# A fused attention and mixture kernel: first batch's q remainder loaded apart and finished late, later batches' loads pinned in the plan, last sub-tile's products, sums and stores rearranged

## The chip, the cores and the metric

The kernel runs on one core of one Trainium2 chip. The metric is the device time of one execution in microseconds (us), median of several runs. A run's time is about 1.8 us more than the span that its profile shows (first to last instruction): the profiled run of the kernel before took 510.41 us and its span is 508.6 us. Below, "time" is the first, "span" the second.

PE is the matrix engine (TensorE), DVE is VectorE, ACT is ScalarE, POOL is GpSimd, SP is SyncE, which here only issues DMAs.

## The reference

```python
# q, k, v: 8 batches, 8 heads, 576 positions, 64 wide
phi = lambda x: where(x > 0, x, exp(x) - 1) + 1
kv  = einsum('bhsd,bhse->bhde', phi(k), v);  z = phi(k).sum(axis=2)
x   = einsum(phi(q), kv) / (einsum(phi(q), z) + 1e-6)     # -> x: 4608 x 512
# mixture: 4 experts, w1 512 x 1024, w2 1024 x 512
p   = domain_probs / (domain_probs.sum(-1) + 1e-9)
out = sum over e of p[:, e] * (relu(x @ w1[e]) @ w2[e])
```

## The kernel before

A batch of 576 positions is cut into 512 and a remainder of 64. The attention goes by pairs of heads, four per batch. Each pair loads k, v and q, takes exp on ACT, maps on DVE, then PE makes kv, the numerators and denominators, and DVE divides. The remainders of k, v and q of a batch are loaded for all heads at once. The first 512 positions go through the four experts while the weights arrive. Everything after that is 64 "units" of 256 rows and one expert: seven block products instead of eight in each layer (a Strassen-like scheme), about 6.18 us of PE each.

Each operation is handed to a small planner with an engine, an assumed duration, a priority and its dependencies. The planner simulates the machine once, at build time, and from that comes one fixed order for each engine.

```python
def order(self):
    ...                                   # pick the engine that can start first
        n = min((n for n, x in cand.items() if x <= t + self.NEAR),
                key=lambda n: (ops[n]["pri"], n))
        start[n] = max(t, at[n])          # at[n]: ready time; begins at o["after"]
        free[e] = done = start[n] + o["dur"]
        if o["move"]:                     # a DMA: assumed time to landing
            mover = max(done + 1.2, mover) + o["move"]
            done = mover + 0.8
    ...                                   # POOL keeps the order of the program
```

For a load of a pair (issue 0.5, move 0.7) the plan thus assumes a landing 0.5 + 1.2 + 0.7 + 0.8 = 3.2 us after the start of the issue when no other DMA is in the way. On the chip no planned time is enforced. Only the order is, and each engine waits at its next instruction until its inputs are there.

The parts that the change touches:

```python
def load_rest(b, queue, pri):                      # k, v, q remainders, together
    for i, (t, o) in enumerate(((k, kqr[rs, 0]), (v, vr[rs]), (q, kqr[rs, 1]))): dma(...)

def rest_maps(b, pe_mode, pri):                    # one exp over k and q together
    pl.add("ACT", 1.05, pri, lambda: nc.scalar.activation(er[rs], kqr[rs], AF.Exp), ...)

def batch(b):                                      # batches 2 to 7, beside the units
    due = U(8 * (b - 1)) - 8                       # U(n) = 84 + 6.4 n
    for pr in range(DC):
        t = due - (DC - pr) * 2 * TU
        load_pair(b, pr, "SP", t - 12)             # a priority only, no earliest time
        if pr == 0:
            load_rest(b, "SP", t - 12); rest_maps(b, False, t - 6)
        attention(b, pr, False, t, 1.7)

# last unit of a sub-tile: seven products, then four sums and the stores
seq = (P1, P4, P5, P2, P6, P7, P3)
ACT: s15 = l2b[0]                                  # after P1 and P5
DVE: of[0:2] = l2b[1] + s1;  of[2] = l2b[3] + of[1]
DVE: of[1,3] = of[1,2] + s5; of[1:3] = l2b[2] + of[1:3]
SP : four stores of 128 KB, one after the other    # last sub-tile
```

Of the kernel before, what the change touches and what calls it, by code (L numbers as in the profile page):

```python
# [109 lines left out]
def kernel(  # L110
# [10 lines left out]
    nc = tc.nc  # L121
# [24 lines left out]
    def sb(name, shape, dt):  # L146
        return pc.tile(shape, dt, tag=name, name=name)

    identh = sb("identh", [P, P], FP16)
    w1_sb = [sb(f"w1_{e}", [P, DC, F], FP16) for e in range(E)]  # L150
# [31 lines left out]
    xr_sb = sb("xr_sb", [P, B // 2, Dm], FP16)  # L182

    kqs.append(
        xp_a.bitcast(FP32).rearrange("p a c (x d) -> p a (c x) d", d=D)
# [35 lines left out]

    def dma(queue, pri, out_, in_, w, move, r=(), hold=False, mark=False):

        eng = nc.gpsimd if queue == "POOL" else nc.sync

        def go():
            i = eng.dma_start(out=out_, in_=in_)
            if mark:
                last["mark"] = i.ins.name
            if hold:  # L230
                tc.add_manual_dep(
                    i.ins,
                    last["mark"],
                    mybir.DependencyInfo(
                        mybir.DependencyClass.Sync, mybir.DependencyReason.DATA
                    ),
                    reason="load order",
                )

        pl.add(  # L240
            queue,
            0.72 if queue == "POOL" else 0.5,
            pri,
            go,
            r=r + (("mark",) if hold else ()),
            w=w + (("mark",) if mark else ()),
            move=move,
        )

    stage = {}  # L250

    def load_pair(b, pr, queue, pri):
        hs = slice(2 * pr, 2 * pr + 2)
        n = 3 if b < 2 else 2
        i = rot("stage%d" % n, n) if n == 2 else rot("stage3", 3)
        stage[b, pr] = i
        kk = stage_keys(i)
        for t, o, key in ((k, kqs[i][:, 0], kk[0]), (v, vss[i], kk[2]), (q, kqs[i][:, 1], kk[1])):
            dma(queue, pri, o, t[b, hs, 0:NT].rearrange("h (p c) d -> p h c d", c=C), (key,), 0.7, hold=b == 2)

    def load_rest(b, queue, pri):
        par = b % 2
        rs = slice(par * R, par * R + R)
        for i, (t, o) in enumerate(((k, kqr[rs, 0]), (v, vr[rs]), (q, kqr[rs, 1]))):
            dma(queue, pri, o, t[b, :, NT:S].rearrange("h s d -> s h d"), (("str", par, i),), 0.75, hold=b in (2, 3))

# [36 lines left out]

    def rest_maps(b, pe_mode, pri):
        par = b % 2
        rs = slice(par * R, par * R + R)
        ei = rot("ek", 2)
        er = ek_b[ei].rearrange("p i h c d -> p i (h c) d")
        ek = (("ek", ei, 0), ("ek", ei, 1))
        s_ = [("str", par, i) for i in range(3)]  # L310

        def maps(i):
            o = kqpr[rs, i]
            nc.vector.tensor_scalar(o, kqr[rs, i], 0.0, 1.0, AO.max, AO.add)
            nc.vector.tensor_tensor(out=o, in0=er[rs, i], in1=o, op=AO.min)

        pl.add("ACT", 1.05, pri, lambda: nc.scalar.activation(er[rs], kqr[rs], AF.Exp),
               r=(s_[0], s_[2]), w=ek)
        pl.add("ACT", 0.55, pri + 0.1,
               lambda: nc.scalar.copy(vprs[par][rs, :, 0:D], vr[rs]), r=(s_[1],), w=(("vpr", par),))  # L320
        for i, key in enumerate(("kpr", "qpr")):
            pl.add("DVE", 0.92, pri + 0.5, lambda i=i: maps(i), r=(s_[0], s_[2]) + ek, w=(key,))
        if not pe_mode:
            pl.add("SP", 0.45, pri + 1, lambda: nc.sync.dma_start_transpose(
                out=qTr[par][:, :, rs], in_=kqpr[rs, 1].rearrange("p h d -> p (h d)")),
                r=("qpr",), w=[("qTr", par, i) for i in range(DC)], move=1.2)

    def attention(b, pr, pe_mode, pri, step, two=False):
# [15 lines left out]
        vp = vps[vi]  # L344
        zi = rot("kvz", 2)
        kvz = kvs[zi]
# [17 lines left out]
        if pe_mode:  # L364

            tq, tk = (l2b[1].bitcast(FP16), "l2b1") if two else (tbank, "l2b3")

            def turn():
                for c in range(C):
                    nc.tensor.transpose(  # L370
                        out=tq[:, c * P : (c + 1) * P], in_=qp[:, c], identity=identh
                    )
                nc.tensor.transpose(
                    out=tq[:, NT : NT + R],
                    in_=kqpr[rs, 1, hs].rearrange("p h d -> p (h d)"),
                    identity=identh[rs, rs],
                )

            pl.add("PE", 0.32, pri + 3 * step, turn, r=(("kqp", pi, 1), "qpr", "ident"),
                   w=(tk,))  # L380
            pl.add("ACT", 0.5, pri + 3.5 * step, lambda: nc.scalar.copy(
                qT.rearrange("p c t -> p (c t)"), tq[:, 0:NT]), r=(tk,), w=(("qT", ti),))
            pl.add("DVE", 0.2, pri + 3.5 * step, lambda: nc.vector.tensor_copy(
                qTr[par][:, pr, rs], tq[:, NT : NT + R]), r=(tk,), w=(("qTr", par, pr),))
        else:
            pl.add("SP", 0.45, pri + 3 * step, lambda: nc.sync.dma_start_transpose(
                out=qT, in_=qp.rearrange("p c h d -> p (c h d)")),
                r=(("kqp", pi, 1),), w=(("qT", ti),), move=1.2)
# [43 lines left out]
        def norm(u, c0, n, ri):  # L432
            nd = at[:, 0 : n * 2 * DE]
            if two and u:
                nd = l2b[2][:, 2 * DE : 6 * DE]
            nd = nd.rearrange("p (c h e) -> p c h e", c=n, h=2)
# [8 lines left out]
            )  # L445
            if c0:
                nc.vector.tensor_tensor(
# [5 lines left out]

        for u, (c0, n) in enumerate(((0, 3), (3, 2))):
            ri = rot("rc", 2)
            pl.add("PE", 0.06 * n, pri + (5 + u) * step, lambda u=u, c0=c0, n=n: nd_mm(u, c0, n),
                   r=(("qT", ti), ("qTr", par, pr), ("kvz", zi)), w=ndk[u])
            pl.add("DVE", (0.72, 0.74)[u], pri + (5.5 + u) * step,
                   lambda u=u, c0=c0, n=n, ri=ri: norm(u, c0, n, ri), r=ndk[u],
                   w=[("x", par, pr, c) for c in range(c0, min(c0 + n, C))]  # L460
                   + ([("xr", b, pr)] if u else []))

# [291 lines left out]
    def l2_unit(n):  # L754
# [25 lines left out]
        P3 = (2, 0, s4[:, 3], Q(3), quad(e, 1, 1), KW(1, 1), False)  # L780
        seq = (P1, P4, P5, P2, P6, P7, P3)
        if first:
            seq = (P1, P5, P2, P6, P7, P4, P3)
        p0 = U(n + 1) + 0.45
        for i, (bank, half, a, ak, w, wk, opens) in enumerate(seq):
            pl.add("PE", 0.436, p0 + 0.9 * i,
                   lambda bank=bank, half=half, a=a, w=w, opens=opens: prod(bank, half, a, w, opens),
                   r=(ak,) + wk, w=lk(bank))
        if not last:
# [7 lines left out]
        s1, s5 = (s15[:, i : i + 1].broadcast_to([P, 2, HD]) for i in range(2))  # L797
        pl.add("ACT", 0.5, p0 + 3.5, lambda: nc.scalar.copy(
            s15.rearrange("p a d -> p (a d)"), l2b[0]), r=("l2b0",), w=("s15",))
        pl.add("DVE", 0.62, p0 + 4.5, lambda: tt(  # L800
# [11 lines left out]
        else:  # L812
            for u in range(2):
                for par in range(2):
                    b = 2 * (2 * s + u) + par
                    dma("SP", p0 + 9, out[b * S + NT : (b + 1) * S, :],
                        ot[par * R : (par + 1) * R, u, :], (), 0.5, r=r)

# [9 lines left out]
    consts(0)  # L828
    pl.add("DVE", 0.8, 5, lambda: consts(1), w=(("vp", 1), ("vpr", 1), ("kvz", 1)))
    for i in range(2):  # L830
        pl.add("DVE", 0.27, 6 + 30 * i, lambda i=i: nc.vector.memset(qTr[i], 0.0),
               w=[("qTr", i, pr) for pr in range(DC)])
    load_pair(0, 0, "SP", 0)
    load_rest(0, "POOL", 0)
    load_pair(0, 1, "POOL", 0)
    load_w1(0, (0,))
    load_pair(0, 2, "POOL", 0)
    load_w1(0, (1,))
    rest_maps(0, True, 3)
    for pr in range(DC):  # L840
        if pr == 3:
            load_pair(0, 3, "POOL", 0)
            load_w1(0, (2, 3))
            probs()
        attention(0, pr, True, 2.5 + 4 * pr, 0.4, two=True)
        turn_x(pr, 6 + 4 * pr)
    load_w2(0)
    load_w1(1, range(DC))
# [28 lines left out]
    def batch(b):  # L877

        due = U(8 * (b - 1)) - 8
        for pr in range(DC):  # L880
            t = due - (DC - pr) * 2 * TU
            load_pair(b, pr, "SP", t - 12)
            if pr == 0:
                load_rest(b, "SP", t - 12)
                rest_maps(b, False, t - 6)
            attention(b, pr, False, t, 1.7)

# [54 lines left out]
```

## Time and profile before

| | before |
|---|---|
| time, first three runs | 508.58 us (508.37 to 508.60) |
| span of the profiled run | 508.6 us |
| PE busy | 484.1 us, 95% |
| first layer 1 product | 16.73 us |
| continuous layer 1 products from | 28.21 us |
| last matmul ends, then the span ends | 501.28, 508.64 us |

The page's summary of busy time of the kernel before:

```profile
span 508.6 us, 14922 instructions
PE 484.1 (95%) x6008; PEld 425.0 (84%) x6008; DVE 410.6 (81%) x1035; ACT 367.1 (72%) x685; POOL 42.6 (8%) x68
```

Busy time does not say how densely PE works, because the records of matmuls overlap: one of 256 columns is 273 ns long (page of before, L765), and the densest start every 109 ns. I therefore worked out a second number from the trace, used all through this document: the "PE excess" of a stretch. It is the sum over matmuls of the time from one start to the next, less what the columns would take at a yardstick of 2.4 per ns, 457.0 us for the whole program. The yardstick is a round number, chosen a little above the densest that the traces show: a product of 512 columns every 0.216 us (2.37 per ns), one of 256 every 0.109 us (2.35). Below, "streaming" is time by this yardstick. So not all excess could be gained: the densest units, after 400 us, take 6.18 us for 5.97 us of streaming. At 0.21 us for each of the 40 units begun between 120 and 380 us, some 8.4 us of excess in that stretch are a floor (an estimate). The first matmul's start, the streaming, the excess and the tail add up to the span.

The timeline of the kernel before, at the start (start us, length us, engine, line, what; in brackets how long the engine was idle and what ended it):

```profile
9.21 1.06 ACT L317 ACTIVATE ek<-kqr 64x1024 f16<-64x1024 f32 x1 [0.30 <-DMA kqr<-in_q_dram]
11.27 0.42 DVE L315 TENSOR_TENSOR kqpr<-ek,kqpr 64x512 f16<-64x512 f16 x1
16.73 1.44 PE L537 MATMUL l1b<-s,w 128*128 128x512 f16 x3 [0.15 <-ACT s L532]
24.02 0.27 DVE L289 TENSOR_REDUCE prs<-p 128x32 f32<-128x128 f32 x1
28.21 1.36 PE L537 MATMUL l1b<-s,w 128*128 128x512 f16 x3 [0.67 <-ACT s L532]
```

The first line is one exp over the k and q remainders, waiting for the q remainder's load. The first layer 1 product comes at 16.73 us, and products run without gaps only from 28.21 us. From 24.02 us DVE does the arithmetic of the probabilities.

The timeline of the kernel before, at the end:

```profile
500.68 0.60 PE L765 MATMUL l2b<-w,s 128*128 128x256 f16 x4
501.30 0.42 DVE L802 TENSOR_TENSOR ot<-l2b,ot 128x256 f32<-128x256 f32 x1
501.75 0.69 DVE L805 TENSOR_TENSOR ot<-ot,s 128x512 f32<-128x512 f32 x1
502.55 0.69 DVE L807 TENSOR_TENSOR ot<-l2b,ot 128x512 f32<-128x512 f32 x1
503.27 2.39 SPq L227 DMA_DIRECT2D out_dram<-ot  x4
```

After the last product DVE still has three sums, then one queue issues four stores in 2.39 us.

ACT's waits in the middle of the kernel before, 120 to 380 us (who waited for whom, total us, times, longest), the four lines in which it waited for DMAs or longest for PE:

```profile
ACT h L703 <- PE l1b L689: 17.4, 17, 2.0
ACT kvz L413 <- PE at L403: 15.1, 15, 1.8
ACT xp L649 <- DMA xT<-xp: 0.6, 2, 0.4
ACT ek L358 <- DMA kq<-in_k_dram: 0.6, 2, 0.4
```

ACT waits for PE there, which is as it should be when PE is the limit, and hardly for loads (0.6 us for k).

### The profile page before, as it was taken

Reading aid. Unit: us, or ns where it says so; the run is one execution under the profiler, and the core shown is the slowest. Engines: PE = TensorE matmul, PEld = TensorE weight load, DVE = VectorE, ACT = ScalarE, POOL = GpSimd, SP = SyncE. Lnnn points to the kernel's source line nnn. Section 1 sums busy time; section 2 is a strip of 40 time slices with the busy share of each in tenths; the row PEclk is TensorE's granted clock in tenths of the full one; section 3 lists DMA queues with packets and bytes.
Section 4 is the critical chain, followed back from the end, with each engine's and each line's share of the span. In section 5 each row is a group of like instructions: output and inputs, shape, how many; then the busy total and the mean of one; then the engine's idle time right before and its main releaser. Section 6 shows DMA issues by size and latency. Waiting matters only on the chain.

```text
span 508.6 us, 14922 instructions
## 1 busy us (share of the span) xinstructions
PE 484.1 (95%) x6008; PEld 425.0 (84%) x6008; DVE 410.6 (81%) x1035; ACT 367.1 (72%) x685; POOL 42.6 (8%) x68
## 2 busy tenths in 40 slices
PE   1889999999999999999999999999999999999994
PEld 0534454889999999999999999999999999999993
DVE  5867897889998989898988989799868676666754
ACT  5636658887987699768977897778666766666640
POOL 8756500000000000000000000000000000000000
PEclk9989999999999999999999999999999999999999
DMA  8999988995775678555665565645322432323311
GB/s 233 227 232 225 262 164 188 234 201 136 162 182 120 138 145 177 121 137 129 175 112 136 124 147 141 108 113 105 95 43 75 54 84 44 84 48 80 51 35 43
DMA packets 124006, 67.51 MB, mean 133 GB/s; under 512 B 94480, under 2 KB 117776, under 8 KB 123936
## 3 DMA queue, kind: packets, MB, share of 16 engines
q1 hardware_dynamic: 115216, 51.79, 46.9%
q0 software_dynamic: 8720, 14.76, 13.7%
q8 instruction: 47, 0.77, 0.7%
q14 instruction: 23, 0.19, 0.1%
HBM read 45.16 MB, written 9.44 MB: 107 GB/s over the span
## 4 chain that ended last, share of the span: by engine, by line
PE 85%; ACT 5%; DMA 4%; DVE 2%; issue 2%; POOL 0%; POOLq 0%; DVEq 0%; ACTq 0%
PE l1b L689 37%; PE l2b L765 36%; PE l2b L547 4%; PE l1b L537 4%; DMA kq<-in_k_dram 2%; PE at L424 2%; PE at L400 1%; DMA kqr<-in_q_dram 1%; ACT xp L649 1%; ACT ek L358 1%; DMA w<-in_moe_w_dram 1%; ACT h L703 1%; ACT l1b L706 1%; ACT p L706 0%; DVE x L440 0%
## 5 line engine op out<-in xcount | busy, mean ns | idle before, releaser
L689 PEld LDWEIGHTS <-w 128*128 128x128 f16 x2048 | 132.9, 98 | 5.6 <-issue 1.0
L765 PE MATMUL l2b<-w,h 128*128 128x256 f16 x768 | 115.1, 273 | 0.3 <-ACT h L703 0.2
L765 PE MATMUL l2b<-t,s 128*128 128x256 f16 x768 | 112.6, 273 | 0.0
L703 ACT ACTIVATE h<-l1b 128x512 f16<-128x512 f32 x128 | 76.7, 599 | 43.1 <-PE l1b L689 41.1
L689 PEld LDWEIGHTS <-w1x 128*128 128x128 f16 x1536 | 100.1, 98 | 5.5 <-issue 2.1
L765 PEld LDWEIGHTS <-s 128*128 128x128 f16 x1024 | 91.2, 98 | 7.1 <-DVE s L751 0.2
L709 DVE CUSTOM_DVE_ANT_0 h<-l1b,p 128x512 f16<-128x512 f32 x64 | 44.2, 691 | 50.1 <-PE l1b L689 48.5
L689 PE MATMUL l1b<-xT,w 128*128 128x128 f16 x1024 | 78.1, 219 | 0.8 <-ACT l1b L706 0.7
L689 PE MATMUL l1b<-xs,w1x 128*128 128x128 f16 x1024 | 77.9, 219 | 0.9 <-DVE h L709 0.4
L689 PE MATMUL l1b<-xs,w 128*128 128x128 f16 x1024 | 78.0, 219 | 0.0
L649 ACT ACTIVATE xp<-x,p_nat 128x512 f16<-128x512 f16 x112 | 76.6, 724 | 0.7 <-DMA xT<-xp 0.6
L765 PEld LDWEIGHTS <-h 128*128 128x128 f16 x768 | 67.3, 98 | 5.4 <-ACT h L703 0.9
L751 DVE TENSOR_TENSOR s<-h 128x512 f16<-128x512 f16 x128 | 53.8, 421 | 1.6
L706 ACT COPY u<-l1b 128x512 f32<-128x512 f32 x64 | 37.5, 586 | 16.0 <-PE l1b L689 15.8
L709 DVE CUSTOM_DVE_ANT_0 h<-l1b,u 128x512 f16<-128x512 f32 x64 | 43.7, 682 | 0.8 <-ACT h L703 0.5
L706 ACT COPY l1b<-l1b 128x512 f32<-128x512 f32 x64 | 36.8, 575 | 10.4 <-PE l1b L689 9.6
L706 ACT COPY p<-l1b 128x512 f32<-128x512 f32 x64 | 37.3, 583 | 7.9 <-PE l1b L689 6.7
L667 DVE TENSOR_TENSOR xs<-xT,xs 128x256 f16<-128x256 f16 x128 | 37.0, 289 | 5.1 <-PE l1b L689 0.5
L358 ACT ACTIVATE ek<-kq 128x512 f16<-128x512 f32 x60 | 37.8, 631 | 3.3 <-DMA kq<-in_k_dram 2.3
L689 PE MATMUL l1b<-xT,w1x 128*128 128x128 f16 x512 | 39.0, 219 | 0.0
L765 PE MATMUL l2b<-w,s 128*128 128x256 f16 x256 | 38.4, 273 | 0.0
L537 PE MATMUL l1b<-s,w 128*128 128x512 f16 x124 | 31.1, 399 | 1.4 <-ACT s L532 1.2
(99 smaller groups left out, 561.0 us busy)
## 6 DMA issues: line engine op xcount, KB each, us to landing
w<-in_moe_w_dram POOLq DMA_DIRECT2D x32, 256.0 KB, 7.3
out_dram<-ot SPq DMA_DIRECT2D x16, 512.0 KB, 2.8
kq<-in_k_dram SPq DMA_DIRECT2D x25, 256.0 KB, 3.3
vs<-in_v_dram SPq DMA_DIRECT2D x25, 256.0 KB, 2.9
kq<-in_q_dram SPq DMA_DIRECT2D x25, 256.0 KB, 3.2
kq<-in_k_dram POOLq DMA_DIRECT2D x5, 256.0 KB, 7.2
vs<-in_v_dram POOLq DMA_DIRECT2D x5, 256.0 KB, 6.6
kq<-in_q_dram POOLq DMA_DIRECT2D x5, 256.0 KB, 6.0
```

Of the source, the lines that this page charges most:

```text
L358: pl.add("ACT", 0.55, pri + i * step, lambda i=i: nc.scalar.activation(ek[:, i], kq[:, i], AF.Exp), r=(sk[i],), w=(("ek", ei, i),))
L424: nc.tensor.matmul(out=nds[u][c - c0], lhsT=qT[:, c] if c < C else qTr[par][:, pr], rhs=kvz, start=True, stop=True,)
L537: nc.tensor.matmul(out=bank, lhsT=w1_sb[e][:, dc, fj * P : (fj + 1) * P], rhs=xt0[:, dc, :], start=(dc == 0), stop=(dc == DC - 1),)
L547: nc.tensor.matmul(out=bank, lhsT=hts[ht[fj]][:, c * P : (c + 1) * P], rhs=w2_sb[e][:, fj, :], start=(fj == 0), stop=(fj == FC - 1),)
L649: pl.add("ACT", 0.55, pri, lambda c=c, src=src, ps=ps: nc.scalar.activation(xp[:, c, :], src, AF.Copy, scale=ps), r=r, w=(("xp", xi, c),))
L667: lambda o=o, a=a, b_=b_: tt(out=o, in0=a, in1=b_, op=AO.subtract),
L689: nc.tensor.matmul(out=bank[:, fc * P : (fc + 1) * P], lhsT=wt[:, kc, fc * P : (fc + 1) * P], rhs=r[:, kc, :], start=(start and fc == 0 an ...
L703: return lambda: nc.scalar.activation(o, bank, AF.Relu)
L706: return lambda: nc.scalar.copy(o, bank)
L709: return lambda: nc.vector._custom_dve(TENSOR_ADD_SAT, out=o, in0=bank, in1=t, s0=BIG, s1=0.0)
L751: pl.add("DVE", 0.36, U(n + 1) + d - 0.5, lambda i=i, a=a, b_=b_, alu=alu: tt(out=s4[:, i], in0=a, in1=b_, op=alu), r=r, w=(Q(i),))
L765: nc.tensor.matmul(out=l2b[bank][:, half * HD : (half + 1) * HD], lhsT=a[:, c, :], rhs=w[:, c], start=(opens and first and c == 0), stop=( ...
```

## The change

Its intent: start the dense work of PE sooner, shorten what follows the last matmul, and move the attention of the later batches to where ACT and DVE have room. The diff, cut to its core (the identity matrix and two more kv buffers are also laid over `s15`, which is free until the first sub-tile's sums, and the exp of the k and q remainders is split in two in all batches):

```diff
-    load_rest(0, "POOL", 0)
+    load_rest(0, "POOL", 0, parts=(0, 1))            # k and v remainders first
     ...
-    rest_maps(0, True, 3)
+    rest_maps(0, True, 3, (0,))
     for pr in range(DC):
         if pr == 3:
             load_pair(0, 3, "POOL", 0)
             load_w1(0, (2, 3))
+            load_rest(0, "POOL", 0, parts=(2,))      # q remainder here
             probs()
         attention(0, pr, True, 2.5 + 4 * pr, 0.4, two=True)   # without the remainder
+    rest_maps(0, True, 30, (1,))
+    rest_late(32)      # turn, products and divisions of all four pairs' remainders
 ...
 def batch(b):
     due = U(8 * (b - 1)) - 8
     for pr in range(DC):
         t = due - (DC - pr) * 2 * TU
-        load_pair(b, pr, "SP", t - 12)
+        if b == 2:
+            t = T0 + 4 + 10.5 * pr
+        load_pair(b, pr, "SP", t - 8, after=t - 8)   # "after": planned no earlier
         if pr == 0:
-            load_rest(b, "SP", t - 12)
-            rest_maps(b, False, t - 6)
-        attention(b, pr, False, t, 1.7)
+            load_rest(b, "SP", t - 7, after=t - 7)
+            rest_maps(b, False, t - 2)
+        attention(b, pr, False, t, 1.5)
 ...
+    elif end:                                        # the last unit of all
+        seq = (P1, P5, P6, P7, P4, P2, P3)
 ...
+    if end:   # six sums, each as soon as its product is there; two stores early,
+              # two at the end, each two from SP and ACT side by side
```

More of the change, by code (lines that the diff above doesn't have):

```diff
@@ L147, in sb @@
         return pc.tile(shape, dt, tag=name, name=name)
-    identh = sb("identh", [P, P], FP16)
     w1_sb = [sb(f"w1_{e}", [P, DC, F], FP16) for e in range(E)]
@@ L182 @@
     xr_sb = sb("xr_sb", [P, B // 2, Dm], FP16)
+    s15h = s15.rearrange("p a d -> p (a d)").bitcast(FP16)
+    identh = s15h[:, 0:P]
+    kvs += [
+        s15h[:, P + i * 2 * DE : P + (i + 1) * 2 * DE].rearrange("p (h e) -> p h e", h=2)
+        for i in range(2)
+    ]
     kqs.append(
@@ L220, with dma @@
     last = {}
-    def dma(queue, pri, out_, in_, w, move, r=(), hold=False, mark=False):
-        eng = nc.gpsimd if queue == "POOL" else nc.sync
+    def dma(queue, pri, out_, in_, w, move, r=(), hold=False, mark=False, after=0.0):
+        eng = {"POOL": nc.gpsimd, "SP": nc.sync, "ACT": nc.scalar}[queue]
         def go():
@@ L247, in dma, with load_pair @@
             move=move,
+            after=after,
         )
     stage = {}
-    def load_pair(b, pr, queue, pri):
+    def load_pair(b, pr, queue, pri, after=0.0):
         hs = slice(2 * pr, 2 * pr + 2)
@@ L258, in load_pair, with load_rest @@
         for t, o, key in ((k, kqs[i][:, 0], kk[0]), (v, vss[i], kk[2]), (q, kqs[i][:, 1], kk[1])):
-            dma(queue, pri, o, t[b, hs, 0:NT].rearrange("h (p c) d -> p h c d", c=C), (key,), 0.7, hold=b == 2)
-    def load_rest(b, queue, pri):
+            dma(queue, pri, o, t[b, hs, 0:NT].rearrange("h (p c) d -> p h c d", c=C), (key,), 0.7,
+                hold=b == 2, after=after)
+    def load_rest(b, queue, pri, after=0.0, parts=(0, 1, 2)):
         par = b % 2
         rs = slice(par * R, par * R + R)
-        for i, (t, o) in enumerate(((k, kqr[rs, 0]), (v, vr[rs]), (q, kqr[rs, 1]))):
-            dma(queue, pri, o, t[b, :, NT:S].rearrange("h s d -> s h d"), (("str", par, i),), 0.75, hold=b in (2, 3))
+        for i in parts:
+            t, o = ((k, kqr[rs, 0]), (v, vr[rs]), (q, kqr[rs, 1]))[i]
+            dma(queue, pri, o, t[b, :, NT:S].rearrange("h s d -> s h d"), (("str", par, i),), 0.75,
+                hold=b in (2, 3), after=after)
     def load_w1(e, dcs):
@@ L301, in probs, with rest_maps @@
                r=(("prawr", 0), ("prawr", 1)), w=("prest",))
-    def rest_maps(b, pe_mode, pri):
+    def rest_maps(b, pe_mode, pri, parts=(0, 1)):
         par = b % 2
@@ L308, in rest_maps @@
         er = ek_b[ei].rearrange("p i h c d -> p i (h c) d")
-        ek = (("ek", ei, 0), ("ek", ei, 1))
-        s_ = [("str", par, i) for i in range(3)]
         def maps(i):
@@ L315, in maps @@
             nc.vector.tensor_tensor(out=o, in0=er[rs, i], in1=o, op=AO.min)
-        pl.add("ACT", 1.05, pri, lambda: nc.scalar.activation(er[rs], kqr[rs], AF.Exp),
-               r=(s_[0], s_[2]), w=ek)
-        pl.add("ACT", 0.55, pri + 0.1,
-               lambda: nc.scalar.copy(vprs[par][rs, :, 0:D], vr[rs]), r=(s_[1],), w=(("vpr", par),))
-        for i, key in enumerate(("kpr", "qpr")):
-            pl.add("DVE", 0.92, pri + 0.5, lambda i=i: maps(i), r=(s_[0], s_[2]) + ek, w=(key,))
+        for i in parts:
+            sk, ek, key = ("str", par, 2 * i), ("ek", ei, i), ("kpr", "qpr")[i]
+            pl.add("ACT", 0.55, pri + i * 0.5, lambda i=i: nc.scalar.activation(
+                er[rs, i], kqr[rs, i], AF.Exp), r=(sk,), w=(ek,))
+            if i == 0:
+                pl.add("ACT", 0.55, pri + 0.1, lambda: nc.scalar.copy(
+                    vprs[par][rs, :, 0:D], vr[rs]), r=(("str", par, 1),), w=(("vpr", par),))
+            pl.add("DVE", 0.92, pri + 0.5 + i * 0.5, lambda i=i: maps(i), r=(sk, ek), w=(key,))
         if not pe_mode:
@@ L326, in rest_maps, with rest_late, turn, mm @@
                 r=("qpr",), w=[("qTr", par, i) for i in range(DC)], move=1.2)
+    def rest_late(pri):
+        rs = slice(0, R)
+        def turn():
+            for pr in range(DC):
+                nc.tensor.transpose(
+                    out=tbank[:, pr * R : (pr + 1) * R],
+                    in_=kqpr[rs, 1, 2 * pr : 2 * pr + 2].rearrange("p h d -> p (h d)"),
+                    identity=identh[rs, rs],
+                )
+        pl.add("PE", 0.22, pri, turn, r=("qpr", "ident"), w=("l2b3",))
+        pl.add("DVE", 0.3, pri, lambda: nc.vector.tensor_copy(
+            qTr[0][:, :, rs], tbank[:, 0 : DC * R].rearrange("p (a t) -> p a t", a=DC)),
+            r=("l2b3",), w=[("qTr", 0, pr) for pr in range(DC)])
+        for p0, n in ((0, 3), (3, 1)):
+            ri = rot("rc", 2)
+            def mm(p0=p0, n=n):
+                for pr in range(p0, p0 + n):
+                    nc.tensor.matmul(
+                        out=slot[pr - p0], lhsT=qTr[0][:, pr], rhs=kvs[pr], start=True, stop=True
+                    )
+            def norm(p0=p0, n=n, ri=ri):
+                nd = at[rs, 0 : n * 2 * DE].rearrange("p (c h e) -> p c h e", c=n, h=2)
+                rc = rc_b[ri][rs]
+                nc.vector.reciprocal(rc[:, 0:n], nd[:, :, :, D:DE])
+                nc.vector.tensor_tensor(
+                    out=xr_sb[rs, 0, p0 * P : (p0 + n) * P].rearrange(
+                        "p (c h d) -> p c h d", c=n, h=2
+                    ),
+                    in0=nd[:, :, :, 0:D],
+                    in1=rc[:, 0:n].broadcast_to([R, n, 2, D]),
+                    op=AO.mult,
+                )
+            prs = range(p0, p0 + n)
+            pl.add("PE", 0.06 * n, pri + 1, mm,
+                   r=[("qTr", 0, pr) for pr in prs] + [("kvz", pr) for pr in prs], w=("at",))
+            pl.add("DVE", 0.25 + 0.16 * n, pri + 1.5, norm, r=("at",),
+                   w=[("xr", 0, pr) for pr in prs])
     def attention(b, pr, pe_mode, pri, step, two=False):
@@ L344, in attention @@
         vp = vps[vi]
-        zi = rot("kvz", 2)
+        zi = pr if two else rot("kvz", 2)
         kvz = kvs[zi]
@@ L372, in turn @@
                     )
+                if two:
+                    return
                 nc.tensor.transpose(
@@ L377, in turn @@
                 )
-            pl.add("PE", 0.32, pri + 3 * step, turn, r=(("kqp", pi, 1), "qpr", "ident"),
-                   w=(tk,))
+            pl.add("PE", 0.32, pri + 3 * step, turn,
+                   r=(("kqp", pi, 1), "ident") + (() if two else ("qpr",)), w=(tk,))
             pl.add("ACT", 0.5, pri + 3.5 * step, lambda: nc.scalar.copy(
                 qT.rearrange("p c t -> p (c t)"), tq[:, 0:NT]), r=(tk,), w=(("qT", ti),))
-            pl.add("DVE", 0.2, pri + 3.5 * step, lambda: nc.vector.tensor_copy(
-                qTr[par][:, pr, rs], tq[:, NT : NT + R]), r=(tk,), w=(("qTr", par, pr),))
+            if not two:
+                pl.add("DVE", 0.2, pri + 3.5 * step, lambda: nc.vector.tensor_copy(
+                    qTr[par][:, pr, rs], tq[:, NT : NT + R]), r=(tk,), w=(("qTr", par, pr),))
         else:
@@ L434, in norm @@
             if two and u:
-                nd = l2b[2][:, 2 * DE : 6 * DE]
+                nd = l2b[2][:, 2 * DE : (2 + 2 * n) * DE]
             nd = nd.rearrange("p (c h e) -> p c h e", c=n, h=2)
@@ L445, in norm @@
             )
-            if c0:
+            if n == 2:
                 nc.vector.tensor_tensor(
@@ L452, in norm @@
                 )
-        for u, (c0, n) in enumerate(((0, 3), (3, 2))):
+        for u, (c0, n) in enumerate(((0, 3), (3, 1 if two else 2))):
             ri = rot("rc", 2)
             pl.add("PE", 0.06 * n, pri + (5 + u) * step, lambda u=u, c0=c0, n=n: nd_mm(u, c0, n),
-                   r=(("qT", ti), ("qTr", par, pr), ("kvz", zi)), w=ndk[u])
-            pl.add("DVE", (0.72, 0.74)[u], pri + (5.5 + u) * step,
+                   r=(("qT", ti), ("kvz", zi)) + ((("qTr", par, pr),) if n == 2 else ()), w=ndk[u])
+            pl.add("DVE", (0.5, 0.74, 0.72)[n - 1], pri + (5.5 + u) * step,
                    lambda u=u, c0=c0, n=n, ri=ri: norm(u, c0, n, ri), r=ndk[u],
                    w=[("x", par, pr, c) for c in range(c0, min(c0 + n, C))]
-                   + ([("xr", b, pr)] if u else []))
+                   + ([("xr", b, pr)] if n == 2 else []))
     out_t = [
@@ L781, in l2_unit @@
         seq = (P1, P4, P5, P2, P6, P7, P3)
+        end = n == nu - 1
         if first:
             seq = (P1, P5, P2, P6, P7, P4, P3)
+        elif end:
+            seq = (P1, P5, P6, P7, P4, P2, P3)
         p0 = U(n + 1) + 0.45
@@ L787, in l2_unit @@
                    lambda bank=bank, half=half, a=a, w=w, opens=opens: prod(bank, half, a, w, opens),
-                   r=(ak,) + wk, w=lk(bank))
+                   r=(ak,) + wk, w=lk(bank) + ((("p", bank, half),) if end else ()))
         if not last:
@@ L797, in l2_unit, with store @@
         s1, s5 = (s15[:, i : i + 1].broadcast_to([P, 2, HD]) for i in range(2))
-        pl.add("ACT", 0.5, p0 + 3.5, lambda: nc.scalar.copy(
-            s15.rearrange("p a d -> p (a d)"), l2b[0]), r=("l2b0",), w=("s15",))
+        sk = ("s15", "ident", ("kvz", 2), ("kvz", 3))
+        if end:
+            for i in range(2):
+                pl.add("ACT", 0.36, p0 + i, lambda i=i: nc.scalar.copy(
+                    s15[:, i], l2b[0][:, i * HD : (i + 1) * HD]), r=(("p", 0, i),),
+                    w=(("s15", i),) + (() if i else sk))
+        else:
+            pl.add("ACT", 0.5, p0 + 3.5, lambda: nc.scalar.copy(
+                s15.rearrange("p a d -> p (a d)"), l2b[0]), r=("l2b0",), w=sk)
+        stores = [(u, par) for u in range(2) for par in range(2)]
+        def store(u, par, queue, r):
+            b = 2 * (2 * s + u) + par
+            dma(queue, p0 + 9, out[b * S + NT : (b + 1) * S, :],
+                ot[par * R : (par + 1) * R, u, :], (), 0.3, r=r)
+        if end:
+            lo, hi = (lambda bank: l2b[bank][:, 0:HD]), (lambda bank: l2b[bank][:, HD : 2 * HD])
+            for dur, o, a_, b_, r, w in (
+                (0.4, of[:, 0], hi(1), s15[:, 0], (("p", 1, 1), ("s15", 0)), (O(0),)),
+                (0.3, of[:, 1], of[:, 0], s15[:, 1], (("s15", 1),), (O(0),)),
+                (0.62, of[:, 2:4], lo(3)[:, None].broadcast_to([P, 2, HD]), of[:, 0:2],
+                 (("p", 3, 0), O(0)), (O(2),)),
+                (0.4, of[:, 2], hi(2), of[:, 2], (("p", 2, 1),), (O(2),)),
+                (0.4, of[:, 0], lo(1), s15[:, 0], ("l2b1",), (O(0),)),
+                (0.4, of[:, 1], lo(2), of[:, 1], lk(2), (O(0),)),
+            ):
+                i = cnt.get("lp", 0)
+                cnt["lp"] = i + 1
+                pl.add("DVE", dur, p0 + 2 + i * 0.5,
+                       lambda o=o, a_=a_, b_=b_: tt(out=o, in0=a_, in1=b_, op=AO.add), r=r, w=w)
+                if i in (3, 5):
+                    for par, queue in enumerate(("SP", "ACT")):
+                        store(int(i == 3), par, queue, (O(2 if i == 3 else 0),))
+            return
         pl.add("DVE", 0.62, p0 + 4.5, lambda: tt(
@@ L812, in l2_unit @@
         else:
-            for u in range(2):
-                for par in range(2):
-                    b = 2 * (2 * s + u) + par
-                    dma("SP", p0 + 9, out[b * S + NT : (b + 1) * S, :],
-                        ot[par * R : (par + 1) * R, u, :], (), 0.5, r=r)
+            for u, par in stores:
+                store(u, par, "SP", r)
     def consts(i):
@@ L829 @@
     pl.add("DVE", 0.8, 5, lambda: consts(1), w=(("vp", 1), ("vpr", 1), ("kvz", 1)))
+    pl.add("DVE", 0.4, 5, lambda: [nc.vector.memset(kvs[i], 0.0) for i in (2, 3)],
+           w=(("kvz", 2), ("kvz", 3)))
     for i in range(2):
```

## The prediction

> **What bounds the kernel now.** The matrix engine (PE): the summary of busy time says 484.1 of 508.6 us (95%), the chain of waits is 85% PE. From 32 to 501.3 us PE is dense: [...] except where the change works:
>
> 1. Start, 0 to 32 us (excess about 18 us). First layer 1 product at 16.73 us, continuous products only from 28.21. The chain runs through the q remainder: it lands at 9.12, one exp over k and q (1.06 us) waits for both, VectorE maps k (ready 10.72), then q, then turn, qT copy, products, x. Later VectorE's probability arithmetic (24.02 to 26.13) stands before the last pair's norm, and PE runs at half clock from 28.3 to 31.7 (512 columns take 427 ns, not 216).
> 2. Main stage's beginning, 84 to 116 us: excess 4.7 us where 1.1 is normal. ScalarE and VectorE are 80 to 90% busy with batch 2's attention and the first units; PE waits for copies.
> 3. Tail: last matmul ends 501.29, sums until 503.24, four stores issued by one queue 503.27 to 505.66, last landing 507.43, end 508.64.
>
> **What the change does.**
> - Start: the q remainder's load leaves the queue's head (1.5 us between landings), its half of the exp (0.5 us), its maps (1.0), and per pair a turn, a 0.19 us copy, a product and a 0.27 us norm leave the pair chain. They come back once, later: about 0.6 us ScalarE, 2.5 VectorE, under 1 PE. Pair 0 then hangs on its q load (8.25): first layer 1 product near 14 us, continuous ones near 24.5. [...] Weights land early enough; tight are batch 1's remainders (41.8 to 43.1). I keep 3.3 us, range 1.5 to 5.5.
> - Main stage: batch 2's loads and attention are planned 5 to 12 us later, off the crowded 80 to 100 us: 1.5 us, range -0.5 to 3. Other batches' later loads cost nothing.
> - Tail: the new product order has its operands in time. Six sums (five of 256 columns, 0.42; one of 512, 0.69) start after the third product and end about 1.15 us after the last matmul instead of 1.95. Two stores go earlier; the last two are issued together, so the last issue begins 1.25 us after the last matmul instead of 3.8. Landing (2.3) and ending (1.2) stay: 2.6 us saved, range 2.1 to 3.
>
> **Sum.** All on the critical path: 3.3 + 1.5 + 2.6 = 7.4; predicted 501.2 us, 8 in 10 within 497.8 to 504.5. Faster by over 2%: 0.17; within: 0.82; slower: 0.01.
>
> **Right or wrong would show as:** first layer 1 product at 13.5 to 15 us; dense PE from 23.5 to 26; first unit's product 3 us earlier than 87.3; excess in 84 to 116 under 3.5; last matmul to end 4.7 us (7.35 before).
>
> **What would make it wrong:** the static order puts the late remainder's turn or norms before work PE needs; load landings in 10 to 50 us (queue saturated) hold the earlier PE back; batch 2's delayed loads starve its units near 135 us; or the probability arithmetic still delays the last pair.

The forecast's sum came to 3.3 + 1.5 + 2.6 = 7.4 us, which takes the median of 508.58 us to 501.2. In the start's paragraph was a reason to hope for up to 1.7 us more, half of the 3.4 us that the trace shows at half clock (28.3 to 31.7 us). The text does not say how much of that is in the 3.3 us or in the range's upper end of 5.5. The excess is defined above, and from 120 to 380 us it is 9.9 us, or 0.76 us per 20 us. Where the text calls a queue saturated, 10 to 50 us, the trace has the DMA engines at a busy share of 1.13 (the packets' time, summed, over the time of 16 engines).

## The result

| | before | changed |
|---|---|---|
| time, first job | 508.59 us (4 runs) | 508.06 us (4 runs, 506.77 to 508.72) |
| time, second job | 508.82 us (11 runs) | 509.03 us (7 runs, 507.94 to 513.09) |
| span, two traces each | 508.6 and 506.7 us | 506.0 and 511.2 us |

The profiled run of before (510.41 us) is none of these; it was 1.8 us above the median of the first three. The ratio of the first job is 0.9986 (95% interval 0.9965 to 1.0007), of the second 0.9994 (0.9972 to 1.0017): the same. A ratio here is the mean time of one kernel's fast runs over that of the other's of the same rounds, so it is not quite the ratio of the medians above. 501.2 us had been predicted, 497.8 to 504.5.

Yet the trace shows the gains. The page's summary and the timeline of the changed kernel, at the start:

```profile
span 506.0 us, 14856 instructions
PE 483.4 (96%) x6008; PEld 424.3 (84%) x6008; DVE 409.1 (81%) x1036; ACT 368.3 (73%) x694; POOL 43.0 (8%) x68
```

```profile
6.51 0.63 ACT L327 ACTIVATE ek<-kqr 64x512 f16<-64x512 f32 x1 [2.15 <-DMA kqr<-in_k_dram]
15.31 1.44 PE L594 MATMUL l1b<-s,w 128*128 128x512 f16 x3 [0.29 <-ACT s L589]
23.93 0.81 PE L594 MATMUL l1b<-s,w 128*128 128x512 f16 x3 [0.68 <-ACT s L589]
```

The exp of the k remainder starts 2.7 us earlier and is shorter, the first product comes 1.4 us earlier and the continuous ones 4.3 us earlier (23.93 for 28.21).

The timeline of the changed kernel at the end:

```profile
499.97 0.60 PE L822 MATMUL l2b<-w,s 128*128 128x256 f16 x4
501.12 0.41 DVE L888 TENSOR_TENSOR ot<-l2b,s 128x256 f32<-128x256 f32 x1
501.23 1.13 SPq L232 DMA_DIRECT2D out_dram<-ot  x2
501.23 1.39 ACTq L232 DMA_DIRECT2D out_dram<-ot  x2
501.45 0.41 DVE L888 TENSOR_TENSOR ot<-l2b,ot 128x256 f32<-128x256 f32 x1
```

The last matmul ends at 500.57 and the span at 506.03, so the tail is 5.46 us where it was 7.36.

So far so good, but the last matmul ends only 0.7 us earlier. The lead over the first trace of before, by the start of each unit's first product (worked out from the timelines):

| unit | 0 | 2 | 8 | 16 | 32 | 44 | 63 |
|---|---|---|---|---|---|---|---|
| lead, us | 5.08 | 9.19 | 5.46 | 4.80 | 2.42 | 0.54 | 0.71 |

(The drop from 9.19 to 5.46 is partly no loss: batch 2's attention was moved into these units, and PE has to do it there. How large that part is was not worked out.) From unit 8 to unit 44 the lead melts away, a little in each batch. ACT's waits of the changed kernel, 120 to 380 us, the lines with a DMA as releaser:

```profile
ACT ek L412 <- DMA kq<-in_q_dram: 3.1, 6, 0.9
ACT ek L412 <- DMA kq<-in_k_dram: 2.6, 4, 1.0
ACT vp L408 <- DMA vs<-in_v_dram: 2.1, 2, 1.2
ACT xp L706 <- DMA xT<-xp: 1.1, 1, 1.1
ACT ek L327 <- DMA kqr<-in_q_dram: 0.5, 1, 0.5
```

Together 9.4 us where it was 1.2 in the kernel before. ACT makes the copies out of PSUM that PE needs, in the same fixed order, so a late load stops these copies as well (in the case below ACT waits 3.46 us for a load, and PE then 3.01 us for a copy). In the changed kernel's first trace 18 matmuls between 120 and 380 us, the first at 128 and the last at 362, start over 0.12 us late by the count of excess. In the first trace of before 3 do. The second trace of the changed kernel (511.2 us) shows one such case in full. SP's issues, then ACT and PE:

```profile
220.87 0.57 SPq L232 DMA_DIRECT2D kq<-in_k_dram  x1
221.50 0.47 SPq L232 DMA_DIRECT2D vs<-in_v_dram  x1
222.02 0.47 SPq L232 DMA_DIRECT2D kq<-in_q_dram  x1
222.58 0.41 SPq L232 DMA_DIRECT2D out_dram<-ot  x1
223.04 0.63 SPq L232 DMA_DIRECT2D kqr<-in_k_dram  x1
223.71 1.48 SPq L232 DMA_DIRECT2D vr<-in_v_dram  x1
225.23 1.41 SPq L232 DMA_DIRECT2D kqr<-in_q_dram  x1
```

```profile
228.81 0.22 PE L481 MATMUL at<-kvz,qTr 128*128 128x130 f16 x1
229.14 0.63 ACT L408 CAST vp<-vs 128x512 f16<-128x512 f32 x1 [3.46 <-DMA vs<-in_v_dram]
231.41 0.57 ACT L763 COPY l1b<-l1b 128x512 f32<-128x512 f32 x1
232.03 0.61 PE L746 MATMUL l1b<-xs,w1x 128*128 128x128 f16 x8 [3.01 <-ACT l1b L763]
232.95 1.06 PE L746 MATMUL l1b<-xT,w 128*128 128x128 f16 x8
```

The v load issued at 221.50 is one of seven DMAs that SP issued within 5.8 us (220.87 to 226.64), one of them a store of 512 KB. ACT waits 3.46 us for it (it landed at 229.12, 7.6 us after the issue), waits another 0.36 us for the q load, then works through an exp, a relu and the copy that PE's next product needs, and PE stands for 3.01 us. This is the worst case of both traces. In the first trace the same load, in the same company, landed in 5.0 us, and PE's starts were late by at most 0.52 us. What made it 2.6 us slower the second time is not shown. After that PE's clock is halved: eight products of 128 columns take 0.85 us (232.95 to 233.80) instead of 0.44. The granted clock of the same run in that stretch (the columns are: stretch, length, then busy us and instructions of PE, PEld, DVE, ACT and POOL, the granted clock, the DMA engines' share and GB/s):

```profile
229.00:232.00 3.00, 0.03 (x1) 0.00 (x0) 0.59 (x2) 2.44 (x5) 0.00 (x0) 1.00 0.09 23
232.00:236.30 4.30, 4.27 (x36) 3.76 (x36) 3.23 (x10) 4.17 (x8) 0.00 (x0) 0.60 0.02 4
```

In this trace ACT kept its order: PE's last layer 1 products before the stall had ended by 228.5 us, yet the relu at 230.78 and the copy at 231.41 us that read such products stood behind the cast at 229.14.

The traces by stretch, in us of PE excess (for "start", the time to the first matmul plus the excess up to 80 us). "Waits" is ACT's idle time of over 0.2 us that a DMA ended, 120 to 380 us, counted by me and so not to the tenth the sum of the views' lines:

| | start | 80-120 | 120-380 | after 380 | tail | waits |
|---|---|---|---|---|---|---|
| before, first trace | 25.2 | 4.9 | 9.9 | 4.1 | 7.36 | 0.9 |
| before, second trace | 22.8 | 5.0 | 10.3 | 4.0 | 7.39 | 1.3 |
| changed, first trace | 20.5 | 3.0 | 15.8 | 4.1 | 5.46 | 9.5 |
| changed, second trace | 20.6 | 3.0 | 20.8 | 4.2 | 5.34 | 12.8 |

### The profile page after: what moved, and what is told of

Same layout as the page of the kernel before. It is cut to its first block, busy times and chain, and to the rows that moved or that the text cites. A ratio compares the mean times of both kernels' runs of the same rounds, so it can differ in the third digit from the quotient of the medians.

```text
span 506.0 us, 14856 instructions
## 1 busy us (share of the span) xinstructions
PE 483.4 (96%) x6008; PEld 424.3 (84%) x6008; DVE 409.1 (81%) x1036; ACT 368.3 (73%) x694; POOL 43.0 (8%) x68
## 4 chain that ended last, share of the span: by engine, by line
PE 72%; ACT 9%; DMA 7%; DVE 7%; issue 4%; SPq 2%; DVEq 0%; POOL 0%; POOLq 0%; ACTq 0%
PE l1b L746 29%; PE l2b L822 28%; PE l1b L594 6%; PE l2b L604 5%; DMA kq<-in_q_dram 2%; ACT xp L706 1%; ACT h L760 1%; SPq L232 1%; DMA kqr<-in_q_dram 1%; PE at L481 1%; DVE s L808 1%; DMA xT<-xp 1%; ACT ek L412 1%; DMA kqr<-in_k_dram 1%; PE at L457 1%
## 5 line engine op out<-in xcount | busy, mean ns | idle before, releaser
L405 DVE TENSOR_TENSOR kqp<-ek,kqp 128x512 f16<-128x512 f16 x64 | 27.2, 425 | 7.7 <-ACT ek L412 3.6
```

The costliest lines, as they stand in the source:

```text
L405: nc.vector.tensor_tensor(out=o, in0=ek[:, i], in1=o, op=AO.min)
```

## The experiments

Theory A: the pinned loads of the later batches, planned close before their use, arrive late on the chip; ACT waits for them in its fixed order, PE starves, and the lead is given back. Theory B: the lead can't be held, whatever the loads do, because ACT, DVE or the DMA engines have no room in the attention stretches. Rival C: the finer steps of 1.5 or batch 2's new place are the cause, and the late loads are only seen beside it.

Every edit of the plan shuffles the fixed order of all engines a little, so a single experiment says less than several that agree. Each run left one trace, and the changed kernel's own two differ by 5.0 us of excess in 120 to 380 us. The ratios, from five or six timed runs of each experiment but two, are therefore the firmer evidence. All differences are below 2%. What tells the experiments from no change is that their 95% intervals do not reach 1.

### All later batches planned as before

The changed kernel with `batch()` of the kernel before (t - 12, no `after`, steps of 1.7, batch 2 not moved).

> The changed kernel with the later batches' loads and attention planned as before (loads 12 us ahead of the attention, steps of 1.7, batch 2 not moved). Theory A (the moved loads of batches 2 to 7 arrive late, ScalarE waits for them in order, PE starves, and the lead won at the start is given back): most of the lead of the start stays, 499 to 503 us. Theory B (the lead is lost whatever the schedule of the loads, as ScalarE, VectorE or the DMA engines can't go faster in the attention stretches): 506.5 to 508.5 us, as the changed kernel.

Measured: 505.12 us, ratio 0.9925 (0.9912 to 0.9938), against 508.81 for before. ACT waits 0.0 us for loads, and the excess in 120 to 380 us is 9.6 us. Theory B falls for that stretch: with the lead at hand the engines keep up there, close to the floor of 8.4 us. The time missed the range of theory A (499 to 503), since 80 to 120 us lost its gain (5.9 us of excess): a stall of 2.42 us at 85.6 us. By the timeline DVE does maps of batch 2's attention there from 79.8 to 82.5 us, then the first batch's four output sums until 85.2, and only then the sums of x (`xs`) for which PE waits. In the changed kernel those of the first unit are done at 78.5 us.

### Loads four microseconds earlier

```diff
-load_pair(b, pr, "SP", t - 8, after=t - 8)       load_rest(b, "SP", t - 7, after=t - 7)
+load_pair(b, pr, "SP", t - 12, after=t - 12)     load_rest(b, "SP", t - 11, after=t - 11)
```

> The changed kernel with the loads of batches 2 to 7 planned 12 us ahead of the attention again instead of 8 (remainders 11 instead of 7), all else as changed, batch 2's place and the steps of 1.5 too. Theory A: the waits of ScalarE for loads between 120 and 380 us (about 8 us in the changed kernel) shrink below 2 us and the time falls to 501 to 504 us. Rival C (the finer steps of 1.5 or batch 2's place cause the stalls, the loads are only seen beside them): stays at 506 to 508.5 us.

Measured: 504.02 us, ratio 0.9912 (0.9898 to 0.9926). The steps of 1.5 and batch 2's place stayed, so rival C falls as the whole cause. The time is at the upper edge of theory A's range (501 to 504). But the waits fell only from 9.5 to 4.3 us, not below 2, and the excess from 15.8 to 13.5 us. By the planner's code, moving a pinned load earlier also lets it place the load's readers earlier. That this is the reason was not measured.

### The old tail

The changed kernel with `end = False`, so that the last unit is handled as before.

> The changed kernel with the last sub-tile's products, sums and stores as before. All theories: the tail is worth the 1.9 us that the two traces show, so 1.5 to 2.3 us slower than the changed kernel: 509.6 to 510.4 us.

Measured: 510.76 us, ratio 1.0046 (1.0021 to 1.0071), a little above the range. In its trace the tail is 7.38 us, 1.9 more than the changed kernel's 5.46. The rest of the difference of the times is in the middle stretch (16.8 us of excess), which differs from run to run.

### The new planning alone

The kernel before with only the new `batch()` and the `after` that it needs.

> The kernel before with only the new planning of batches 2 to 7 (loads 8 us ahead, steps of 1.5, batch 2 moved). Theory A: it gains up to 3.5 us in 84 to 116 us and loses about 6 us after 120 us: 510 to 513 us. Theory B: without the early start there is no lead to lose: 505 to 508.6 us.

Measured: 515.17 us (511.63 to 516.77), ratio 1.0110 (1.0082 to 1.0137). In its trace 80 to 120 us gains 2.1 us (2.8 for 4.9) and 120 to 380 us loses 6.6 us (16.5 for 9.9), with 7.8 us of waits for DMAs. The new planning makes the kernel slower without any early start, and by more than theory A had said (510 to 513). The profiled run took 512.79 us and four of the five others longer, so these figures are rather its milder case.

### Batch 2 as changed, batches 3 to 7 as before

```diff
             if b == 2:
                 ...                                  # as in the changed kernel
+                continue
+            load_pair(b, pr, "SP", t - 12)
+            if pr == 0:
+                load_rest(b, "SP", t - 12)
+                rest_maps(b, False, t - 6)
+            attention(b, pr, False, t, 1.7)
```

> The changed kernel with batch 2 planned as changed (moved, pinned loads) and batches 3 to 7 as before (loads not pinned, 12 us ahead, steps of 1.7). Theory A (just-in-time loads of batches 3 to 7 give the lead back): the lead of about 9 us at the third unit is kept but for some 3 us of batch 2's own deferred work, under 2 us of PE stalls after 150 us, 501 to 503.5 us, faster than both kernels and than the run with all batches as before (505.1). Theory B (the lead can't be held): 505 to 508.

Measured: 506.80 us, ratio 0.9953 (0.9934 to 0.9971). This is a miss: theory A had said 501 to 503.5, and the time lies where theory B had it (505 to 508). The waits fell to 2.3 us, but the excess in 120 to 380 us is still 12.9 us and in 80 to 120 us it is 4.5. SP issued seven pairs' k loads between 95 and 140 us, where the changed kernel issued four: batch 3's unpinned loads ran ahead into the stretch of batch 2's moved attention. The count alone does not explain the loss: the run with all loads unpinned issued six there and lost less. That the two batches then got in each other's way is an argument, not shown. It does show that late loads are not the only way for this plan to lose time.

### Slack in the plan, loads pinned as changed

```diff
-                done = mover + 0.8
+                done = mover + 0.8 + o["lag"]        # lag = 3.0 for loads of batches 2 to 7
```

> The changed kernel, loads pinned as changed, but the planner is told that each load of batches 2 to 7 lands 3 us later than it assumed, so it places the work that reads them that much later in each engine's order. Theory A in its sharper form (pinned loads are planned just in time with a landing near 3 us after issue where the trace shows 3.8 median and 5.4 at the ninth tenth; the order has no slack): ScalarE's waits for loads fall from 9.5 to under 3 us, PE stalls after 92 us from 6.5 to under 3, 502 to 505 us. Rival C (the lateness of the work itself, or the steps of 1.5, cost the time): 507 us or more.

Measured: 505.71 us, ratio 0.9930 (0.9911 to 0.9950). The time misses the range (502 to 505) by 0.7 us, but it is 3.3 us below the changed kernel in the same job (509.03). This is the sharpest test: the loads keep their pins, and only the place of the work that reads them moves. The waits fell from 9.5 to 0.8 us, the excess in 120 to 380 us from 15.8 to 12.8 us. The stalls of PE over 0.12 us after 92 us fell from 6.5 to 4.3 us in all, where under 3 had been expected. So the missing slack of the readers was a cause, and it accounts for ACT's waits. A part of the loss stays under this edit though ACT hardly waits for loads, and what causes that part is not shown.

### Loads not pinned

```diff
-load_pair(b, pr, "SP", t - 8, after=t - 8)       load_rest(b, "SP", t - 7, after=t - 7)
+load_pair(b, pr, "SP", t - 12)                   load_rest(b, "SP", t - 12)
```

> The changed kernel with the loads of batches 2 to 7 not pinned (no earliest time, priority 12 us ahead); batch 2's place, steps of 1.5 stay. Theory A: the loads run ahead as their buffers come free, ScalarE's waits for them between 120 and 380 us fall from 9.5 us to under 2, 501 to 504 us. Rival C (steps of 1.5 or batch 2's place): 506 to 508.5.

Measured: 505.12 us, ratio 0.9914 (0.9894 to 0.9933). Waits 1.0 us, excess in 120 to 380 us 10.8 us, with batch 2's new place and the steps of 1.5 kept. The time is 1.1 us above the range; the excess of 80 to 120 us rose from 3.0 to 4.6 us. Compare the "us to landing" of the q loads, DMA issues part of the page, changed kernel first, then this one:

```profile
kq<-in_q_dram SPq DMA_DIRECT2D x25, 256.0 KB, 4.0
```

```profile
kq<-in_q_dram SPq DMA_DIRECT2D x25, 256.0 KB, 3.1
```

Pinned, the q loads are also slower in the median, above the 3.2 us that the plan assumes (3.9 to 4.2 in the six traces with all of them pinned). Unpinned they took 3.1 to 3.3 in six traces, but 3.6 in the second of before. The k and v loads of the changed kernel, at 3.0 and 3.2, were not above it.

### The changed kernel again

> The changed kernel once more on the same chip, as a measure beside the others: 506.5 to 509 us, 0.995 to 1.001 of before, with ScalarE waiting about 9 us for loads between 120 and 380 us.

Measured: 509.03 us, ratio 0.9994, at the upper edge of the range. The profiled run took 513.09 us, above the range, as did two others (510.38, 510.57); its waits are 12.8 us, with the stall and the half clock shown above.

### The kernel before again

> The kernel before, once more, for a second trace. The first trace (span 508.6 us) ran PE at half clock from 28.3 to 31.7 us, and timed runs of this kernel fall in two groups, granted clock 0.994 (509.2 to 510.8 us) and 0.995 to 0.998 (508.0 to 508.8). If the half clock there is chance, this trace may lack it: span near 506.8 us, PE excess in 0 to 80 us near 18.3 us instead of 20.0.

Measured: one run of 508.43 us, span 506.7 us. The half clock is gone. The stretch of 28 to 32 us in the first trace of before and in this one:

```profile
28.00:32.00 4.00, 3.79 (x10) 1.40 (x10) 3.32 (x6) 2.49 (x6) 2.71 (x4) 0.57 1.18 207
```

```profile
28.00:32.00 4.00, 3.96 (x20) 1.71 (x18) 2.89 (x5) 3.45 (x8) 1.73 (x3) 1.00 1.20 205
```

The same program did 10 matmuls at a granted clock of 0.57 and 20 at 1.00. So the first trace of before, on which the prediction was built, was a bad throw of about 2 us (1.7 of them are half of the 3.4 us at half clock), and the profile pair of 508.6 and 506.0 us overstates the change. Continuous products begin at 27.21 us in the second trace, not 28.21. The start's share is 2.3 us against the second trace of before, not 4.7. That the first trace was a slow one could be seen before: its run took 510.41 us, and the prediction took gains read from it off the median of 508.58. Timed runs agree on the whole: of the 11 runs of before in one job, the five at a mean clock of 0.994 took 509.2 to 510.8 us, the six above it 508.0 to 508.8. (In another job two of three runs at 0.994 took 508.9 and two at 0.996 took 509.4 and 509.7, so the mean clock alone doesn't separate them.)

### Not pinned, and slack in the plan

The loads as in "Loads not pinned", with a `lag` of 2.0.

> A try for a better version: the changed kernel, loads of batches 2 to 7 not pinned, and the planner told that they land 2 us later. Theory A: ScalarE's waits for loads under 1 us, PE excess in 120 to 380 us below 11 us (15.8 in the changed kernel's trace), 503 to 505 us. If slack only moves work to worse places: 505 to 507.

Measured: 503.18 us (502.82 to 504.15), ratio 0.9893 (0.9877 to 0.9908), against 508.64 for before. This is faster than both kernels, by about 1%. The waits are 0.5 us. Excess: start 22.1 (1.6 us more than the changed kernel's, which was not looked into), 80 to 120 us 3.8, 120 to 380 us 9.5, tail 5.88. All of ACT's waits for DMAs in its trace, 120 to 380 us:

```profile
ACT ek L413 <- DMA out_dram<-ot: 0.5, 1, 0.5
ACT xp L707 <- DMA xT<-xp: 0.2, 1, 0.2
```

Where the changed kernel waited 8.3 us for loads of k, v and q, this one shows none. (The releaser of the first line is inferred; an exp reads no output, so it may be another DMA of the same semaphore.)

### The start alone

The changed kernel with the old `batch()` and the old tail.

> The start alone: the changed kernel with the old planning of batches 2 to 7 and the old tail. The start is worth about 3 us against runs of before without the half clock, less 1 us of PE excess in 80 to 120 us: 506.5 to 507.5 us, and about 1.9 us more than the run with the new tail (505.1).

Measured: 507.15 us, ratio 0.9969 (0.9955 to 0.9984), 2.0 us above the run with the new tail, as expected. The stretches around its stall at 85 us:

```profile
83.00:85.60 2.60, 0.66 (x12) 0.65 (x12) 2.53 (x7) 2.58 (x5) 0.00 (x0) 1.00 1.11 212
85.60:89.00 3.40, 3.40 (x37) 3.40 (x34) 2.98 (x8) 3.07 (x7) 0.00 (x0) 0.50 0.93 256
```

The same stall of 2.42 us is in the traces of three kernels that share this order; the half clock followed in two of them (this one and the next) and not in the third (all later batches as before).

The clock records of the traces show a difference between them. In the traces the changes of the clock lie on a grid with a step of 3.41 us (in the first trace of before 21.50, 28.32, 31.74 and 506.19 us, in the first of the changed kernel 18.45 and 503.15, 142 steps apart). Here the clock changes at 17.37, 85.63 and 89.05 us, and from the first to the second it is 20 steps. The step from 82.22 to 85.63 us holds the whole stall, and products stream in it for only 0.95 us. In the third trace a step ends at 83.61 us, in the middle of the stall, and neither step beside it streams less than 1.31 us. By my count over all 14 traces, from the first full clock (at 17 to 22 us) until the last products, four steps have 0.81 to 1.18 us of streaming, each followed by half clock, and none of the others, from 1.31 us up, was. (The one in the first trace of before is the step from 24.91 to 28.32 us, with 1.18 us; the lowest of its other steps has 1.76 us.) In these three traces the half clock thus went with how the steps lay over the same stall. More about its cause is not shown.

### One queue for the last stores

The kernel of "All later batches planned as before", with all four last stores issued from SP.

> The changed kernel with the old planning of batches 2 to 7, and the last four stores all issued from one queue. From the last matmul's end to the end of the span the changed kernel takes 5.46 us, the kernel before 7.36. If the second queue saves issue time: 5.9 to 6.2 us. If the stores' landing is bound by their transfer: 5.4 to 5.6 us.

Measured: one run of 505.51 us. The tail is 6.03 us, and 5.39 with two queues, so the second queue saves 0.64 us. The last issue came 2.44 us after the last matmul instead of 1.32, 1.12 us later, but landed in 2.37 us instead of 2.79. The slow landings with two queues are those of ACT's stores (2.65 and 2.78 us). SP's, issued at the same moments, took 2.31 and 2.32, and ACT's last issue lasted 0.73 us where SP's lasted 0.47. So two queues saved 1.12 us of issue time, and 0.42 us came back in ACT's landing. Why ACT's stores landed later is not shown; SP's stores beside them were not slower.

## Why the prediction was wrong

It predicted 501.2 us (497.8 to 504.5) and 508.06 was measured. The terms of its sum, beside the traces of the changed kernel's first run and the second of before (without the half clock), whose spans differ by 0.6 us:

| term | predicted | measured |
|---|---|---|
| start | 3.3 | 2.3 (22.8 to 20.5 us; 4.7 against the first trace) |
| main stage's beginning, 80 to 120 us | 1.5 | 2.0 (5.0 to 3.0 us) |
| later batches' loads and new places, 120 to 380 us | 0 | -5.5 (10.3 to 15.8 us; -10.5 by the changed kernel's second trace) |
| tail | 2.6 | 1.9 (7.39 to 5.46 us) |
| sum | 7.4 | 0.7 |

- The step that failed is the sentence "Other batches' later loads cost nothing." It took the PE's rhythm in 120 to 380 us as given and the four microseconds as slack. The runs showed a cost of 5.5 us there. Pinned loads have their readers placed by an assumed landing of 3.2 us, the chip took 4.0 us in the median for the q loads and 7.6 in the worst case shown, and ACT, which reads them, also makes the copies that PE waits for. Giving slack alone (0.9930), unpinning alone (0.9914), both (0.9893) and the old planning (0.9925) each won time back. Of the 5.5 us, by one trace each, slack alone gave back 3.0 and unpinning alone 5.0, so the pins cost more than the waits of ACT that slack removes. The prediction had named "batch 2's delayed loads starve its units near 135 us" as what might make it wrong. That was the right mechanism, but it is all of batches 2 to 7, with the 18 late starts of PE between 128 and 362 us.
- The start was right in its mechanism and in two of its three marks: dense products from 23.93 us (23.5 to 26 predicted) and a first unit 5.1 us earlier in the first traces (3 predicted). The first product at 15.31 us missed the 13.5 to 15 predicted. Part of this rested on a half clock at 28.3 us that was an accident of the trace; 2.3 us is what a trace without it shows. The prediction hoped to avoid it by denser work, for a reason not shown by these traces. The half clock lasted 3.41 us, but PE had not been idle before it: in the 3.41 us before it products streamed for 1.18 us, and no gap was over 0.80 us.
- The main stage's beginning was right: 2.4 us of excess from 84 to 116 us, predicted under 3.5, and 4.7 before.
- The tail was right in mechanism and mis-sized in one term. The last issue began 1.32 us after the last matmul (1.25 predicted). The landing, taken over as 2.3 us, took 2.86 for the last store, which ACT issued; SP's, issued at the same moment, took 2.33. So the tail took 5.46 us in place of 4.7. It is the second queue that the prediction had too cheap, by about 0.5 us. That the stores overlap is not the reason: the four from one queue overlapped too and landed in 2.24 to 2.37.
- The other dangers named did not come true: 20 to 80 us shows no long stall, and the late remainder's work cost the dense products nothing that shows.

What stays open is the loss in the run with only batch 2 moved, and the 2.5 us of excess in 120 to 380 us that the run with slack alone keeps over the second trace of before (12.8 against 10.3).

## What to carry to other kernels

A fixed order made from a model is only as good as the model's latencies: leave several microseconds between a load's assumed landing and the place of its reader, above all on an engine that also feeds the bottleneck (here 3.0 us of slack took ACT's waits for DMAs from 9.5 to 0.8 us). When a start is made earlier, follow the lead unit by unit to the end, since it may be won and given back in different places. Take a second trace of the kernel before, before putting a number on a stage of it.
